# A first softmax in two pieces with a share on GpSimd, a first y copied by PSUM banks, and one softmax piece moved forward

## The chip, the cores and the metric

The kernel runs on one core of one Trainium2 chip. The metric is the device time in microseconds (us), the median over runs of one launch. The engines are TensorE (PE; its weight loads are PEld), VectorE (DVE), ScalarE (ACT), GpSimd (POOL) and SyncE (SP, which here only issues DMAs).

## The reference, cut to what matters

A causal dynamic convolution with softmax weights over 7 taps, 8 heads of 24 columns, then two dense layers with a squared ReLU between them.

```python
w = softmax(weight_gen, axis=-1)              # (8, 4096, 8 heads, 7 taps)
out[b, s, h, :] = sum_k w[b, s, h, k] * x_pad[b, s + k, h, :]
h = np.maximum(out.reshape(32768, 192) @ w_in, 0.0)       # 192 x 2048
result = h * h @ w_out                                    # 2048 x 192
```

## The kernel before

The sequence is cut into blocks of 512 or 1024 positions. For each block, DVE multiplies rows of softmax weights (`wr`) by a mask into band matrices (`bd`). PE multiplies bands by x into PSUM (`yp`), and a copy to `y` follows. PE then multiplies y by `w_in` into `h`, ACT takes ReLU to `t`, DVE squares to `g`, and PE multiplies by `w_out` into `o`. ACT copies and DVE adds `o` into `o_sb`. The first softmax part covers the first 1024 positions.

```python
        def exp(self, lo, hi):            # ACT
            ...
            nc.scalar.activation(out=self.ex[:, lo:hi]..., in_=self.wg[:, lo:hi]..., func=ActF.Exp)

        def total(self, lo, hi):          # DVE: sums over the taps
            nc.vector.tensor_reduce(out=self.ssum[:, lo:hi]..., in_=self.ex[:, lo:hi]..., ...)

        def scale(self, lo, hi, eng):
            while lo < hi:
                n = min(SL - lo % SL, hi - lo)
                for g in range(HP):       # 4 pairs of heads
                    eng.tensor_tensor(out=..., in0=self.ex[:, lo : lo + n, g],
                                      in1=self.rcp[:, lo : lo + n, g]..., op=AluOp.mult)
                lo += n
...
        # st_conv(j): the first y is copied in three pieces, two of them of one bank
            copies = ((k0, k1, nc.scalar.copy),)
            if j == 0:
                copies = ((0, 1, nc.scalar.copy),) + tuple(
                    (k, k + 1, nc.vector.tensor_copy) for k in range(1, NK)
                )
...
        s0.load(nc.sync)                                  # weights of the first softmax
        load_w_in(w_st[0], 0, nc.sync)
        x_load_f32(0)
        load_w_in(w_st[1], 1, nc.sync)
        s0.exp(0, s0.rh)
        s0.total(0, s0.rh)
        s0.recip(0, s0.rh)
        s0.scale(0, s0.rh, nc.vector)
        nc.scalar.copy(out=w_i[:, 0, 0], in_=w_st[0])
        wr_load_sbuf(0, [s0], (0, 2, 1, 4, 3), (nc.sync, nc.gpsimd))   # moves of softmax rows
        wr_load_sbuf(1, [s0], range(NT), (nc.gpsimd,))
        x_cast(0, nc.scalar.copy)
        cross_w_in_by_pe(0)
        spin(14)                                          # matmuls that keep the clock up
        x_load_f32(1)
        nc.scalar.copy(out=w_i[:, 1, 0], in_=w_st[1])
        cross_w_in(1)
        s1.load(nc.sync)
        for i in (0, 2, 1, 3, 4):
            st_band(0, (i,))
        st_conv(0)
...
        # later: plans say after which unit ("u") an exp (E), a softmax piece (S),
        # bands (B), a half of the second layer (M) or the next convolution (C) comes
            3: "L5 L6 M S3 u u u M u u u u M u M B6 E4 u u u M M B7 u u u M u M C S4 u",
...
        TIMES = {
            (1, 0): ((3, 15), (4, 1)),    # part 4: second piece after unit 1 of block 4
```

The softmax here doesn't subtract the row's maximum and nothing guards it: scores larger than these inputs give would overflow.

## Time and profile before

| | |
|---|---|
| time, median of 4 runs | 748.41 us (747.88 to 750.02) |
| span of the profiled run | 746.1 us |
| PE busy | 738.3 us, 99% |
| chain that ended last | 94% PE, 3% DVE, 1% each DMA and ACT |
| DVE, ACT, POOL busy | 621.9, 624.1, 88.9 us |
| first matmul of the second layer | 25.82 us |
| PE's one shown wait for an engine after that | 0.48 us at 89.29 us |

A busy PE is not a PE at its peak, but what an edit can win without touching matmuls lies where PE waits. The prediction shows those places. Two of them count here: the start, where a chain of single steps leads to the first convolution, and one wait near 89 us. In a line of the timeline the two first numbers are start and length, and the bracket at the end is the engine's idle time ahead of it and what ended that time.

### The profile page before, as it was taken

What the parts mean: (1) busy time and instruction counts of PE and PEld (TensorE: products, weight loads), DVE (VectorE), ACT (ScalarE), POOL (GpSimd) and SP (SyncE); (2) the same over time, 40 slices, a digit from 0 to 9 for tenths busy, and PEclk for the clock granted to TensorE, in tenths of its full rate; (3) what the DMA queues carried; (4) which work ended last, traced back from release to release, by engine and by line L of the source; (5) the groups of instructions that cost most, each with busy time, mean ns of one, the idle gap of its engine ahead of it and who ended that gap; (6) DMA issues with size and microseconds to landing.
All of it is one profiled execution on the core that took longest, in us unless ns stands there. A gap on an engine that the chain in (4) does not pass through costs nothing.

```text
span 746.1 us, 33290 instructions
## 1 busy us (share of the span) xinstructions
PE 738.3 (99%) x15106; PEld 558.0 (75%) x15106; DVE 621.9 (83%) x1003; ACT 624.1 (84%) x755; POOL 88.9 (12%) x130
## 2 busy tenths in 40 slices
PE   8999999999999999999999999999999999999998
PEld 4767777777777797777877777787777777777787
DVE  5999898998889888887889888898888987677853
ACT  5998888898888888888888888888888888888884
POOL 7322220101101100011000110001100011000000
PEclk9999999999999999999999999999999999999999
DMA  8755444435554244643146442265341354442312
GB/s 218 118 100 115 80 93 93 99 71 139 94 118 80 72 59 80 140 83 71 39 78 139 98 69 61 43 139 108 59 80 47 58 108 80 60 73 51 51 45 66
DMA packets 122170, 64.81 MB, mean 87 GB/s; under 512 B 83850, under 2 KB 118637, under 8 KB 121517
## 3 DMA queue, kind: packets, MB, share of 16 engines
q1 hardware_dynamic: 77708, 45.66, 22.3%
q0 software_dynamic: 44176, 16.93, 20.1%
q8 instruction: 118, 1.93, 1.0%
q14 instruction: 24, 0.19, 0.1%
q10 hardware_dynamic: 144, 0.10, 0.0%
HBM read 48.61 MB, written 28.70 MB: 104 GB/s over the span
## 4 chain that ended last, share of the span: by engine, by line
PE 94%; DVE 3%; DMA 1%; ACT 1%; issue 1%; DVEq 0%; ACTq 0%
PE o L482 45%; PE h L448 43%; PE yp L416 6%; DVE bd L348 1%; DVE g L460 1%; DMA wr<-v_first 0%; DMA wg<-in_weight_gen_dram 0%; ACT t L457 0%; DVE v_first L239 0%; DVE ssum L224 0%; DVE rcp L231 0%; ACT ex L217 0%; DVE o_sb L498 0%; ACT y L434 0%; ACT o_sb L496 0%
## 5 line engine op out<-in xcount | busy, mean ns | idle before, releaser
L457 ACT ACTIVATE t<-h 128x1024 f16<-128x1024 f32 x512 | 496.7, 1026 | 64.8 <-PE h L448 64.4
L460 DVE TENSOR_TENSOR g<-t 128x1024 f16<-128x1024 f16 x512 | 333.9, 686 | 99.6 <-ACT t L457 97.0
L482 PEld LDWEIGHTS <-g 64*128 64x128 f16 (+1 forms) x8032 | 351.5, 94 | 55.0 <-issue 4.1
L482 PE MATMUL o<-w_o,g 64*128 64x192 f16 (+1 forms) x8032 | 383.9, 243 | 0.5 <-DVE o_sb L498 0.5
L448 PE MATMUL h<-y,w_i 64*128 64x512 f16 (+1 forms) x3168 | 378.7, 370 | 1.7 <-ACT t L457 0.8
L448 PEld LDWEIGHTS <-w_i 64*128 64x128 f16 x3168 | 163.5, 94 | 114.8 <-issue 5.0
L348 DVE TENSOR_TENSOR bd<-wr,mask 128x4160 f16<-128x4160 f16 (+3 forms) x89 | 149.3, 1701 | 3.7 <-DMA wr<-v_first 3.7
L300 POOL DMA_DIRECT2D xt<-in_x_dram x62 | 51.6, 836 | 443.0 <-PE yp L416 420.1
L496 ACT COPY o_sb<-o 128x384 f32<-128x384 f32 x129 | 62.3, 483 | 33.9 <-PE o L482 33.9
L498 DVE TENSOR_TENSOR o_sb<-o,o_sb 128x384 f32<-128x384 f32 x123 | 68.2, 554 | 8.4 <-ACT o_sb L496 5.6
L434 ACT CAST y<-yp 128x1024 f16<-128x1024 f32 (+1 forms) x64 | 47.7, 796 | 15.0 <-PE yp L416 15.0
L416 PE MATMUL yp<-bd,xt 128*32 128x104 f16 (+8 forms) x3864 | 51.8, 208 | 0.6 <-DVE bd L348 0.3
L416 PEld LDWEIGHTS <-xt 128*32 128x32 f16 (+3 forms) x3864 | 46.1, 91 | 7.0 <-issue 6.4
L217 ACT ACTIVATE ex<-wg 128x448 f32<-128x448 f32 (+2 forms) x44 | 27.2, 618 | 1.9 <-DMA wg<-in_weight_gen_dram 1.9
L239 DVE TENSOR_TENSOR v_big<-ex,rcp 128x112 f16<-128x112 f32 (+1 forms) x136 | 27.3, 263 | 1.6 <-DMA vd<-v_big 0.4
L224 DVE TENSOR_REDUCE ssum<-ex 128x64 f32<-128x448 f32 (+2 forms) x44 | 26.1, 593 | 2.4 <-ACT ex L217 2.4
L231 DVE RECIPROCAL rcp<-ssum 128x64 f32<-128x64 f32 (+2 forms) x44 | 23.7, 539 | 1.5
L290 POOL DMA_DIRECT2D xt<-in_x_dram x7 | 3.8, 548 | 137.2 <-PE yp L416 137.2
L330 POOL DMA_DIRECT2D wr<-v_first x31 | 16.8, 559 | 18.3 <-DVE v_first L239 18.1
L546 PE MATMUL wp<-warm 128*128 128x512 f16 x39 | 10.5, 434 | 1.3 <-DVE warm L538 1.3
L546 PEld LDWEIGHTS <-warm 128*128 128x128 f16 x39 | 4.2, 110 | 6.9 <-issue 2.4
L239 DVE TENSOR_TENSOR v_first<-ex,rcp 128x112 f16<-128x112 f32 (+1 forms) x48 | 9.1, 255 | 0.3
(25 smaller groups left out, 28.6 us busy)
## 6 DMA issues: line engine op xcount, KB each, us to landing
out_dram<-o_sb SPq DMA_DIRECT2D x63, 384.0 KB, 2.9
xt<-in_x_dram POOLq DMA_DIRECT2D x42, 240.0 KB, 5.7
wg<-in_weight_gen_dram SPq DMA_DIRECT2D x4, 1064.0 KB, 8.2
xt<-in_x_dram POOLq DMA_DIRECT2D x20, 192.0 KB, 5.4
wr<-vd SPq DMA_DIRECT2D x38, 80.0 KB, 3.7
vd<-v_big SPq DMA_DIRECT2D x5, 512.0 KB, 5.5
wg<-in_weight_gen_dram SPq DMA_DIRECT2D x5, 392.0 KB
wg<-in_weight_gen_dram SPq DMA_DIRECT2D x3, 616.0 KB, 4.5
```

The lines of the kernel that those rows point to most:

```text
L217: nc.scalar.activation(out=self.ex[:, lo:hi].rearrange("p r g k e -> p (r g) k e"), in_=self.wg[:, lo:hi].rearrange("p r (g e) k -> p (r g ...
L239: eng.tensor_tensor(out=bass.AP(tensor=v.tensor, offset=v.offset + lo * H * SL + lo % SL * 2 + g * SL * 2, ap=[list(v.ap[0]), [H * SL + 2, ...
L300: eng.dma_start(out=dst[:, first:last], in_=ap)
L348: nc.vector.tensor_tensor(out=bd_t[j][:, H * lo : H * (lo + len(tiles) * n)].rearrange("p (g m c) -> p g m c", g=shape[1], c=2 * SL), in0= ...
L416: nc.tensor.matmul(out=yps[k // per][p0 : p0 + m, col + a : col + b], lhsT=x_t[s][:, i, 32 * q : 32 * q + m], rhs=bd[:, h // 2, h % 2, a - ...
L434: copy(out=y[:, a:b, 0:th], in_=yp[:, (a - k0) * th : (b - k0) * th].rearrange("p (k c) -> p k c", c=th),)
L448: nc.tensor.matmul(out=h[:, half, jj * th : (jj + 1) * th], lhsT=w_in_chunk(u * per + jj, slot, half), rhs=y_t[j][r0 : r0 + RT, k, 0:th], ...
L457: nc.scalar.activation(out=t1, in_=h, func=ActF.Relu)
L460: nc.vector.tensor_tensor(out=g, in0=t1, in1=t1, op=AluOp.mult)
L482: nc.tensor.matmul(out=oo[:, cc * Dm : (cc + 1) * Dm], lhsT=g[r0 : r0 + n, cc * P : (cc + 1) * P], rhs=w_o[r0 : r0 + n, fc, :], start=(fc ...
L496: nc.scalar.copy(out=o_sb, in_=o[0][:, c])
L498: nc.vector.tensor_tensor(out=o_sb, in0=o[1][:, c], in1=o_sb, op=AluOp.add)
```

## The change

It means to shorten the start and take away that wait. The sums begin after the first part of exp (8 of the 14 rows that a partition holds) instead of after all of it, GpSimd does a quarter of the scaling, ACT and DVE each copy one PSUM bank of the first y, and the second piece of part 4's softmax comes one unit sooner.

```diff
-        def scale(self, lo, hi, eng):
+        def scale(self, lo, hi, eng, pairs=range(HP)):
...
-                for g in range(HP):
+                for g in pairs:
...
-                copies = ((0, 1, nc.scalar.copy),) + tuple(
-                    (k, k + 1, nc.vector.tensor_copy) for k in range(1, NK)
-                )
+                copies = ((0, 2, nc.scalar.copy), (2, NK, nc.vector.tensor_copy))
...
-        s0.exp(0, s0.rh)
-        s0.total(0, s0.rh)
+        for lo, hi in ((0, FIRST), (FIRST, s0.rh)):
+            s0.exp(lo, hi)
+            s0.total(lo, hi)
         s0.recip(0, s0.rh)
-        s0.scale(0, s0.rh, nc.vector)
+        s0.scale(0, s0.rh, nc.vector, range(HP - 1))
+        s0.scale(0, s0.rh, nc.gpsimd, (HP - 1,))
...
-            3: "... M M B7 u u u M u M C S4 u",
+            3: "... M M B7 u u u E4 M u M C S4 u",
...
-            (1, 0): ((3, 15), (4, 1)),
+            (1, 0): ((3, 15), (4, 0)),
```

## The prediction

> **What bounds the kernel now.** I read the page first, its busy shares and the chain of work that ended last.
>
> ```profile
> PE 738.3 (99%) x15106; PEld 558.0 (75%) x15106; DVE 621.9 (83%) x1003; ACT 624.1 (84%) x755; POOL 88.9 (12%) x130
> PE 94%; DVE 3%; DMA 1%; ACT 1%; issue 1%; DVEq 0%; ACTq 0%
> ```
>
> The span is 746.1 us, and 94% of the chain is TensorE (PE): two dense layers, back to back. The edit leaves every matmul as it is. It can only win where PE waits, so I looked for PE's holes with the table of busy time by stretch: PE is busy 8.10 of the 10 us from 15 to 25, 9.52 of 10 us from 80 to 90, and 579.96 of 580 us from 140 to 720. The first 25 us, which include the fill, and one hole near 89 us are all that is on offer. The end, 23.18 of 26 us, isn't touched.
>
> Next, the chain of waits in order of time through the start; columns are start, length, what.
>
> ```profile
> 0.82 3.13 DMA wg<-in_weight_gen_dram
> 3.98 0.94 ACT ex L217
> 4.94 0.98 DVE ssum L224
> 5.95 0.86 DVE rcp L231
> 6.83 1.47 DVE v_first L239 x8
> 8.31 3.57 DMA wr<-v_first
> 11.98 2.61 DVE bd L348 x5
> ```
>
> Every step is serial: the load, exp, sums, reciprocal, scaling, the move of rows, then the bands that the first convolution multiplies by. Lastly the timeline of the first y copy and what follows, by engine.
>
> ```profile
> 15.11 0.37 ACT L434 CAST y<-yp 128x256 f16<-128x256 f32 x1 [1.94 <-PE yp L416]
> 15.51 0.75 DVE L434 CAST y<-yp 128x256 f16<-128x256 f32 x2 [0.93 <-ACT y L434]
> 15.99 2.91 PE L448 MATMUL h<-y,w_i 64*128 64x256 f16 x47 [0.19 <-DVE y L434]
> 16.97 2.85 ACT L457 ACTIVATE t<-h 128x1024 f16<-128x1024 f32 x3 [1.49 <-PE h L448]
> ```
>
> VectorE (DVE) starts its copies when ScalarE (ACT) has ended its own: they share a bank for the second third of y. PE gets its y piecewise and stalls between. From 16.97 ACT runs without a hole until 27.8 us; PE waits for it at 21.61 and then takes over as the bound at 25.06, where the chain turns into PE alone. So the start saves what the first ACT pass on h, now at 16.97, moves forward.
>
> The hole near 89 us, again in the timeline:
>
> ```profile
> 79.57 0.69 DVE L460 TENSOR_TENSOR g<-t 128x1024 f16<-128x1024 f16 x1 [0.49 <-ACT t L457]
> 81.34 0.69 DVE L460 TENSOR_TENSOR g<-t 128x1024 f16<-128x1024 f16 x1 [1.08 <-ACT t L457]
> ...
> 88.69 0.55 DVE L498 TENSOR_TENSOR o_sb<-o,o_sb 128x384 f32<-128x384 f32 x1
> 89.29 1.48 PE L482 MATMUL o<-w_o,g 64*128 64x192 f16 x31 [0.48 <-DVE o_sb L498]
> ```
>
> DVE idles 1.08 us before 81.34, then runs two softmax pieces (82.58 to 84.3 and 84.83 to 87.0) that delay its o_sum at 88.69. PE waits 0.48 us for it. ACT's half of that o_sum ended by 87.31 (86.83 + 0.48), so DVE is at fault.
>
> **What the Trainium skill says.** "SBUF — State Buffer", section "Who interferes with whom": a DVE instruction with two SBUF inputs contends with a GpSimd instruction that reads SBUF, and the loser blocks. The split scaling is exactly this pair. No GpSimd instruction with two inputs is in this trace, so it neither agrees nor disagrees. "GPSIMD Engine Reference", section "3.1 Elementwise — side-by-side cycle accounting", gives 4497 ns for a tensor_tensor add of 2048 fp32 elements; again there is none here. "PSUM — Partial Sum Buffer", section "PSUM bank collisions raise a hardware error", has it that two engines may not be in the same bank and quadrant at once. The trace agrees as far as it can: DVE sat idle 0.93 us until ACT's y copy had ended. "DMA: Bandwidth & Descriptors", section "Queues, rings and completion order", says that a DMA engine consumes one ring's descriptors in order. The trace fits: the first row move landed after 3.57 us, behind the large weight loads of the same queue, where moves from the softmax buffer take 1.7 us at least and 2.2 in the median over the first 30 us.
>
> **The change, part by part.**
>
> Exp and sums in two pieces. By the rows with shapes kept apart, 448 elements of exp take 633 ns and 336 take 525; the sums take 608 and 494. ACT's instructions overlap by some 0.11 us (three of 1.026 in 2.85) and DVE's scaling ones by some 0.08. Exp ends at 3.98 + 0.63 = 4.61 and at 4.61 - 0.11 + 0.53 = 5.03. The first sums run from 4.63 to 5.24, the second from 5.16 to 5.65. The reciprocal starts at about 5.68 for 5.95 and the scaling at 6.58 for 6.83: 0.25 us won.
>
> Scaling shared with GpSimd. DVE keeps 6 of 8 instructions: 1.47 x 6/8 = 1.10 us, so it ends at 7.68 for 8.30. GpSimd gets one of 112 and one of 84 elements. My estimate from the GPSIMD page: 4497/2048 = 2.2 ns an element, plus 0.1 us each for starting (its 1-element memsets take 0.10 in the trace), gives 0.35 + 0.28 = 0.63 us. It clears v_big until 6.99 (4.55 + 2.44), so alone it would end at 7.62. If each blocks the other fully, both end at 6.58 + 1.10 + 0.63 = 8.31, and the saving of the first part is lost. I take the middle, 8.0: the row moves are issued 0.3 us earlier.
>
> Does the landing follow? The large piece of the second weight half is issued at 4.07 and lands 6.9 us later, at 10.97; the first rows land at 11.88. The DMA engines are at 90% or more from 5.5 to 9.6 us. I let half through: bands start 0.15 us earlier. The warming matmuls ahead of the convolution don't eat this: the last of 14 starts at 12.79, and PE then waits for bands (0.28 us at 14.13).
>
> The y copy by banks. ACT copies 512 columns, 592 ns by its row of that shape, from 15.11 to 15.70, and DVE the other bank from 15.11 to 15.53. The first h then starts at 15.73 with all of y. Before, its first matmul stood at 15.53, the next at 15.99, and the third pair of operands was only there at 16.27 (15.51 + 0.75 and some). A pass of 12 such matmuls takes 0.76 in the chain; 15.73 + 0.76 = 16.49, with 0.15 us to reach ACT 16.64 for 16.97: 0.33 us won. DVE comes free 0.7 us earlier too, but the second convolution's y copy isn't waiting for it, because ACT is busy.
>
> The softmax piece of part 4. Its exp (525 ns) moves into the block before, where ACT has a hole of 0.84 us, and its sums, reciprocal and scaling one unit forward. They take 1.72 us (82.58 to 84.3) and now fall into DVE's idle 1.08 us. DVE's o_sum at 88.69 comes about 1.1 us earlier, 87.6, and is gated then by ACT at 87.31. PE wanted it at 88.81 (88.57 + 0.24), so the whole 0.48 us goes; I count 0.45.
>
> Sum: 0.15 + 0.33 + 0.45 = 0.93 us of 748.18, or 747.2.
>
> **The rivals.** First, the port pair: GpSimd and DVE block each other, the scaling ends at 8.3 or later, and part one is worth nothing. For it speaks the skill; against it, GpSimd starts late, with part of DVE's work done. It leaves 747.4. Second, the row moves are hidden behind the weight loads whatever the softmax does; the 10.97 landing speaks for it, that moves are short and the loads nearly drained by 9.6 against it. This too gives 747.4. Third, ACT meets the next softmax load: the part-1 weights are requested at 14.40 as before and exp starts at 19.70 without a shown wait. If they land only shortly before, the y copy's 0.33 us turns into a wait there, giving 747.6 or so. Fourth, the softmax shift: if the earlier exp or the later g (0.7 us at 81.34) makes PE wait elsewhere, some 0.3 us returns. If all that is good goes right (rows follow fully, GpSimd is unhindered: 0.6 for 0.15), 746.7.
>
> **Range and chances.** Mechanisms span about 746.7 to 748.2. The three runs of before lie from 747.88 to 750.02, so a median can be off by some tenths. I predict 747.2 us, with 746.1 to 748.4 holding it 8 times in 10. Two per cent would be 15 us; PE's idle time in the whole span is 746.1 - 738.3 = 7.8 us, so faster by over 2% is out of reach (0.005), and nothing in the edit can add 15 us (0.005): within 2%, 0.99.
>
> **What would show it.** Of the changed kernel: scaling ends between 7.7 and 8.3, with GpSimd's two instructions from about 7.0; the first row move still lands near 11.7; DVE's single y copy starts with ACT's at about 15.0; the first ACT pass on h starts near 16.5 and PE's unbroken stretch 0.5 us earlier than 25.06; PE no longer waits for o_sum near 89 us, and DVE's idle 1.08 us is filled. The prediction is wrong if a new PE wait stands in blocks 3 to 5, if the landing moves by a whole half microsecond or goes back, or if exp of part 1 shows a DMA wait.

## The result

| | before | after |
|---|---|---|
| time, median of 4 runs | 748.41 us | 747.93 us (747.22 to 748.56) |
| ratio | | 0.9990, 95% interval 0.9972 to 1.0008 |
| span of the profiled run | 746.1 us | 746.3 us |

The ratio is the mean time of one kernel's runs over that of the other's runs of the same rounds, so it isn't quite the ratio of the medians. Its interval contains 1: the time alone doesn't show a gain. The traces have to.

The page of the changed kernel, busy shares and chain:

```profile
PE 738.4 (99%) x15106; PEld 560.4 (75%) x15106; DVE 622.1 (83%) x1001; ACT 624.4 (84%) x756; POOL 89.4 (12%) x132
PE 95%; DVE 2%; ACT 1%; DMA 1%; issue 1%; DVEq 0%; ACTq 0%; SPq 0%
```

PE is the bound as before. The chain of waits through the start of the changed kernel (start, length, what):

```profile
4.14 0.63 ACT ex L217
...
4.79 1.04 DVE ssum L224 x2
...
5.86 0.86 DVE rcp L231
...
6.74 1.46 DVE v_first L239 x6
...
8.28 3.24 DMA wr<-v_first
...
11.62 2.61 DVE bd L348 x5
```

The reader should compare lengths. Six scaling instructions on DVE take 1.46 us, as eight did before (1.47), and the row move is issued at 8.28 for 8.31: exp took less, but it began 0.16 us later in this run, behind its load. Yet the bands start at 11.62 for 11.98, because the move took 3.24 us for 3.57. That difference isn't the softmax's doing, as the experiments show. The timeline of the first y copy in the changed kernel, ACT, DVE and PE:

```profile
14.74 0.58 ACT L432 CAST y<-yp 128x512 f16<-128x512 f32 x1 [1.92 <-PE yp L416]
...
15.36 0.42 DVE L432 CAST y<-yp 128x256 f16<-128x256 f32 x1 [1.15 <-ACT y L432]
...
16.49 2.85 ACT L455 ACTIVATE t<-h 128x1024 f16<-128x1024 f32 x3 [1.16 <-PE h L446]
```

DVE's copy of the second bank still begins when ACT's has ended. From the start of the y copy to the first ACT pass on h it is 16.49 - 14.74 = 1.75 us for 1.86 (16.97 - 15.11): 0.11 us won, not 0.33. Last, the place of the old wait, DVE and PE of the changed kernel:

```profile
79.40 0.69 DVE L458 TENSOR_TENSOR g<-t 128x1024 f16<-128x1024 f16 x1 [0.51 <-ACT t L455]
80.01 0.50 DVE L224 TENSOR_REDUCE ssum<-ex 128x48 f32<-128x336 f32 x1
...
93.40 0.55 DVE L496 TENSOR_TENSOR o_sb<-o,o_sb 128x384 f32<-128x384 f32 x1
...
93.63 1.85 PE L480 MATMUL o<-w_o,g 64*128 64x192 f16 x32
```

The softmax piece now runs at 80.01 in what was an idle stretch, and PE's wait at 89 is gone. But a group of 32 matmuls that takes 1.48 us elsewhere takes 1.85 at 93.63: PE waits there for DVE's o_sum at 93.40, behind two bands. In the terms of the 0.48 us of before this is 0.13 us of idle time: the group's first matmul ends at 93.87 and the next starts at 94.00.

Both kernels keep the same instructions from the sixth block on. From its convolution (the *arrival*, 99.19 us before and 98.67 after) to the last block's, the trace has 609.81 us before and 610.66 after. So the changed kernel came 0.52 us sooner to the steady stretch and lost 0.85 us in it, which is why its span is no shorter. The 0.52 us add up, to 0.01: the first matmul of the second layer came 0.46 us sooner (25.36 for 25.82), the fifth block took 0.32 us less, and the fourth, from its convolution to the fifth's, took 0.25 more (22.85 for 22.60). That loss in the fourth block doesn't belong to the change: the second trace of the changed kernel has 22.60 there (e10).

### The profile page after: what moved, and what is told of

The parts are those of the page before. It is cut to its first block, busy times and chain, and to the rows that moved or that the text cites. A ratio compares the mean times of both kernels' runs of the same rounds, so it can differ in the third digit from the quotient of the medians.

```text
span 746.3 us, 33293 instructions
## 1 busy us (share of the span) xinstructions
PE 738.4 (99%) x15106; PEld 560.4 (75%) x15106; DVE 622.1 (83%) x1001; ACT 624.4 (84%) x756; POOL 89.4 (12%) x132
## 4 chain that ended last, share of the span: by engine, by line
PE 95%; DVE 2%; ACT 1%; DMA 1%; issue 1%; DVEq 0%; ACTq 0%; SPq 0%
PE o L480 45%; PE h L446 43%; PE yp L416 6%; ACT t L455 1%; DVE bd L348 1%; DMA wg<-in_weight_gen_dram 0%; DMA wr<-v_first 0%; DVE g L458 0%; ACT ex L217 0%; DVE v_first L239 0%; DVE ssum L224 0%; DVE o_sb L496 0%; DVE rcp L231 0%; ACT y L432 0%; DVE y L432 0%
## 5 line engine op out<-in xcount | busy, mean ns | idle before, releaser
L446 PEld LDWEIGHTS <-w_i 64*128 64x128 f16 x3168 | 166.2, 94 | 112.8 <-issue 4.1
```

Source lines behind the costliest of these rows:

```text
L446: nc.tensor.matmul(out=h[:, half, jj * th : (jj + 1) * th], lhsT=w_in_chunk(u * per + jj, slot, half), rhs=y_t[j][r0 : r0 + RT, k, 0:th], ...
```

## The experiments

Twelve experiments ran, on two chips. Each is given by its difference from the changed kernel unless said otherwise. A table of what the traces show comes first; all times are us from the start of the span. "Weights" is the landing of the large piece of the second weight half, "rows" the issue of the first row move on SP, "bands" the start of the first band. "y to h" runs from the start of the y copy to ACT's first pass on h, "fifth" from the fifth block's convolution to the sixth's, "steady" from the arrival to the last convolution.

| kernel | weights | rows | bands | y to h | fifth | arrival | steady |
|---|---|---|---|---|---|---|---|
| before | 11.02 | 8.31 | 11.98 | 1.86 | 23.24 | 99.19 | 609.81 |
| before again (e8) | 11.95 | 8.33 | 12.85 | 1.86 | 23.26 | 100.02 | 610.86 |
| after | 10.36 | 8.28 | 11.62 | 1.75 | 22.92 | 98.67 | 610.66 |
| after again (e10) | 10.89 | 8.20 | 12.14 | 2.17 | 22.90 | 99.90 | 610.99 |
| e1, scaling on DVE | 10.51 | 8.09 | 11.80 | 1.74 | 22.90 | 98.51 | 611.91 |
| e2, two y tiles | 10.76 | 8.08 | 11.66 | 1.50 | 22.92 | 98.62 | 611.92 |
| e3, no shift | 11.05 | 8.11 | 11.97 | 1.74 | 23.18 | 99.14 | 611.33 |
| e6, e1 and e2 together | 10.65 | 8.30 | 11.83 | 1.50 | 22.92 | 98.33 | 610.33 |
| e12, e6 again | 10.94 | 8.10 | 11.89 | 1.51 | 22.91 | 98.31 | 610.35 |
| e7, scaling on GpSimd | 11.11 | 9.63 | 11.82 | 1.74 | 22.91 | 99.32 | 610.09 |

### e1 and e7: who does the scaling

Theory: the two engines block each other, so GpSimd's quarter buys nothing. Rival: it helps, and something else hid it.

```diff
-        s0.scale(0, s0.rh, nc.vector, range(HP - 1))
-        s0.scale(0, s0.rh, nc.gpsimd, (HP - 1,))
+        s0.scale(0, s0.rh, nc.vector)        # e1
+        s0.scale(0, s0.rh, nc.gpsimd)        # e7
```

> The changed kernel with the whole first scaling back on VectorE (8 instructions), all else kept. Theory (the two engines block each other, GpSimd's share is bought back in full): from the start of the first exp to the end of the scaling 4.05 us as with the split, +-0.05, because 8 unhindered VectorE instructions take 1.45 us and 6 hindered ones took 1.45 too; GpSimd issues its first row move about 0.3 us after the scaling instead of 0.67. Rival (the split does help, something else in that run hid it): the scaling takes 0.2 to 0.4 us longer than with the split. Time within 0.5 us of the changed kernel either way.

> The changed kernel with the whole first scaling on GpSimd, VectorE idle: it measures GpSimd's instruction by itself. Theory (with the split, each engine was blocked while the other read): GpSimd's instruction of 112 elements takes 0.33 to 0.40 us from start to start, that of 84 0.26 to 0.32, for 0.45 with the split; the whole scaling about 2.7 us. Rival (GpSimd isn't blocked, it is simply this slow, and only VectorE was blocked): 0.45 us from start to start. Time not asked.

The groups of instructions around the scaling, shapes kept apart (busy us, mean ns of one). First the changed kernel, GpSimd and DVE:

```profile
L239 POOL TENSOR_TENSOR v_first<-ex,rcp 128x112 f16<-128x112 f32 x1 | 0.5, 478 | 0.0
L239 POOL TENSOR_TENSOR v_first<-ex,rcp 128x84 f16<-128x84 f32 x1 | 0.4, 360 | 0.0
...
L239 DVE TENSOR_TENSOR v_first<-ex,rcp 128x112 f16<-128x112 f32 x3 | 0.8, 336 | 0.0
L239 DVE TENSOR_TENSOR v_first<-ex,rcp 128x84 f16<-128x84 f32 x3 | 0.7, 280 | 0.0
```

e1, DVE alone:

```profile
L239 DVE TENSOR_TENSOR v_first<-ex,rcp 128x112 f16<-128x112 f32 x4 | 0.8, 270 | 0.0
L239 DVE TENSOR_TENSOR v_first<-ex,rcp 128x84 f16<-128x84 f32 x4 | 0.7, 240 | 0.0
```

e7, GpSimd alone:

```profile
L239 POOL TENSOR_TENSOR v_first<-ex,rcp 128x112 f16<-128x112 f32 x4 | 1.4, 387 | 0.0
L239 POOL TENSOR_TENSOR v_first<-ex,rcp 128x84 f16<-128x84 f32 x4 | 1.2, 342 | 0.0
```

DVE's instruction is longer when GpSimd works: 336 ns for 270 on average. In the changed kernel the stretching stands instruction by instruction: DVE's third takes 464 ns while GpSimd's first runs, and its fourth 377 for 240 while GpSimd's second runs. GpSimd's first is longer too in this trace, 478 ns for 387. But in the second trace of the changed kernel (e10), where DVE's third and fourth took 464 and 379 ns again, it is not:

```profile
L239 POOL TENSOR_TENSOR v_first<-ex,rcp 128x112 f16<-128x112 f32 x1 | 0.4, 392 | 0.0
L239 POOL TENSOR_TENSOR v_first<-ex,rcp 128x84 f16<-128x84 f32 x1 | 0.4, 360 | 0.0
```

So DVE is held up in both traces, and GpSimd not in each: that the two block each other is shown for one side only. From the start of exp to the end of the scaling it is 4.05 us with the split, 4.06 on DVE alone (e1) and 4.31 before. So two pieces of exp gave 0.25 us, and GpSimd gave nothing. In e7 GpSimd's instructions start 0.35 and 0.29 us apart and the whole scaling takes 2.62 us, near the 2.7 that the theory had.

The split has a small cost too: GpSimd's first row move follows the scaling by 0.67 us with it, by 0.31 before and by 0.31 in e1. In the first trace of the changed kernel DVE waited 0.57 us for the second block's rows, which are all moved by GpSimd. The other traces of this order with the split (e2, e3 and e10) have no such wait, so it isn't a steady cost.

The time of e1 was 748.03 us for 748.93 before, ratio 0.9992 (0.9977 to 1.0007), unclear as was expected.

### Does the landing follow? e4, e7 and e8

Theory: the first rows queue behind the weights on the DMA engines, so a softmax that ends sooner gains nothing. Rival: the landing follows the issue, wholly or by half as the prediction had it. e4 issues the second weight half behind the first three row moves.

```diff
         x_load_f32(0)
-        load_w_in(w_st[1], 1, nc.sync)
...
         wr_load_sbuf(0, [s0], (0, 2, 1, 4, 3), (nc.sync, nc.gpsimd))
+        load_w_in(w_st[1], 1, nc.sync)
```

> The changed kernel with the load of the second weight half issued behind the three first row moves of the same queue. It is a test of what sets the landing of the rows; it should cost time, as the weights then come late (0.5 to 2 us). Theory (the rows queue behind the weight loads): first row move lands 2.0 to 2.6 us after its issue for 3.24 and 3.57. Rival (a move of 128-byte rows takes 3.2 us by itself): 3.0 us or more.

The timeline of DVE, the line of the first bands, in e4:

```profile
10.27 2.60 DVE L348 TENSOR_TENSOR bd<-wr,mask 128x832 f16<-128x832 f16 x5 [2.17 <-DMA wr<-v_first]
```

In e7, where the rows are issued 1.5 us later than in e1:

```profile
11.82 2.60 DVE L348 TENSOR_TENSOR bd<-wr,mask 128x832 f16<-128x832 f16 x5 [5.19 <-DMA wr<-v_first]
```

In e8, the kernel before run again:

```profile
12.85 2.60 DVE L348 TENSOR_TENSOR bd<-wr,mask 128x832 f16<-128x832 f16 x5 [4.54 <-DMA wr<-v_first]
```

With the weights out of the way the first move lands 2.0 us after its issue and bands start at 10.27. With the weights ahead, bands start at 11.82 whether the rows are issued at 9.63 (e7) or near 8.1 (11.80 in e1). In e8 the same program as before, its rows issued at 8.33, has its weights 0.93 us later and its bands 0.87 us later. The weights of e7 landed even later than those of e1 (11.11 for 10.51), so they can't have made up for the late issue. So the end of the softmax has about 1.5 us of slack in this pair, and the 0.36 us by which the changed kernel's bands came sooner go with weights that landed 0.66 us sooner in that one run. They don't go with the issue: among the nine traces of the table that issue the rows from 8.08 to 8.33, an issue at 8.28 has the soonest bands (11.62) and one at 8.10 has 11.89. Nor do they follow the weights to the tenth: from landing to bands it is 0.71 to 1.29 us. The prediction's second rival is shown.

e4 cost 6 us (754.94, ratio 1.0083, 1.0069 to 1.0096), more than the 0.5 to 2 expected: ACT converts the late weights ahead of the y copy, which then began at 17.98 us, and PE, idle meanwhile, had a granted clock of 0.50 from 18 to 21 us.

> The kernel before, unchanged, as if it were a change: it shows what two sets of runs of one program differ by, and a second trace of it. Expected: ratio 1.000 with an interval of some +-0.15%, so that a gain of 0.4 us (0.05%) can't be seen in the time; landing of the weights' large piece and of the first rows moved together by up to 0.4 us against the first trace; 1.86 us from the y copy's start to the first pass on h and PE's wait near 89 us as before; PE's losses after 100 us different from the first trace by up to 1 us.

e8 gave 749.39 us against 749.16 of the same program in the same rounds, ratio 1.0009 (0.9995 to 1.0022): two sets of one program can differ by 0.09%, or 0.7 us. In its trace the start moved by 0.9 us where 0.4 was expected.

### e2: why DVE waits with its y copy

The program as built has DVE's copy wait on an ACT semaphore, although the two copies read different banks. Both read one PSUM tile. e2 gives each bank a tile.

```diff
+        if j == 0:
+            per = 2                     # one PSUM tile for each bank
         yps = [
             ps_h.tile([P, 2 * TB], f32, name="yp", tag="h") for _ in range(-(-NK // per))
         ]
...
-                copies = ((0, 2, nc.scalar.copy), (2, NK, nc.vector.tensor_copy))
+                copies = ((k0, k1, (nc.scalar.copy, nc.vector.tensor_copy)[n]),)
```

> The changed kernel with the first y's two banks as two PSUM tiles instead of one, copies as before. Theory (VectorE waits for ScalarE because both copies read one tile, not because of a bank): VectorE's copy now starts with ScalarE's (within 0.1 us), PE's first dense matmuls run without the wait for the third part of y, and the first ScalarE pass on h starts 0.25 to 0.3 us sooner after the end of the convolution: about 1.5 us after it for 1.77. Rival (the two engines' reads are kept apart for the y tile they write, or the pass waits for something else): no change, 1.77 us. Whole time 0.3 us less at most, which the timing hardly shows.

The program as built now has that copy wait on PE. The timeline of ACT and DVE in e2:

```profile
14.75 0.58 ACT L434 CAST y<-yp 128x512 f16<-128x512 f32 x1 [1.92 <-PE yp L418]
16.25 1.94 ACT L457 ACTIVATE t<-h 128x1024 f16<-128x1024 f32 x2 [0.92 <-PE h L448]
...
14.81 0.42 DVE L434 CAST y<-yp 128x256 f16<-128x256 f32 x1 [0.55 <-PE yp L418]
```

DVE now starts 0.06 us after ACT, and it is 1.50 us to the first pass on h: 0.25 less than with one tile and 0.36 less than before. The rival falls: it was neither a bank nor the y tile. The time was 749.02 us, ratio 1.0000 (0.9987 to 1.0013). The trace shows part of why: PE later waited for bands near 33 us, whose rows landed until 29.6 us in this run. What held them was not tested.

### e3: the softmax shift

```diff
-            3: "... M M B7 u u u E4 M u M C S4 u",
+            3: "... M M B7 u u u M u M C S4 u",
-            (1, 0): ((3, 15), (4, 0)),
+            (1, 0): ((3, 15), (4, 1)),
```

> The changed kernel with the second exp and softmax piece of part 4 back where they were. Theory: PE's wait of 0.48 us for o_sum near 88 us returns, VectorE's idle 1.08 us returns before it, and the stretch from one convolution to the next there takes 23.2 us for 22.9. Rival (that wait was gone for the earlier start of everything, or chance): no PE wait there. Time up by 0.3 to 0.5 us, near what the timing resolves.

The timeline of PE in e3:

```profile
89.24 1.48 PE L480 MATMUL o<-w_o,g 64*128 64x192 f16 x31 [0.41 <-DVE o_sb L496]
```

The wait returns, and with it 23.18 us for the fifth block. Three traces without the shift have 23.18 to 23.26 there, all eleven with it 22.90 to 22.94: 0.32 us between the two means. The wait that vanished was 0.41 to 0.48 us; 0.13 us of it came back as the idle time near 94 us, in all eleven traces. The time, 749.81 us and ratio 1.0016 (1.0002 to 1.0030), is worse than this accounts for: 1.2 us by the ratio, where the trace explains 0.3. Its steady stretch was 1.5 us longer than that of the first trace of before, with the same instructions.

### e6 and e12: scaling on DVE with two y tiles

> As the last, without moving the weight pieces: scaling on VectorE, the first y in two PSUM tiles. It asks whether the 0.5 us that the two-tile run lost after its better start (bands of the third block waited for rows until 29.6 us) is its own or chance. Theory (chance, the loads of that stretch were late in that one run): first pass on h 1.5 us after the y copy's start again, and no wait of PE for bands near 33 us; arrival at the sixth block's convolution 98.2 to 98.4. Rival (the earlier VectorE work makes GpSimd's loads late): the loss of about 0.5 us near 33 us is back, arrival 98.6 or later.

> The version with the scaling on VectorE and the first y in two PSUM tiles again, to see whether its gain over the kernel before repeats: ratio 0.998 to 1.000, 1.5 us from the y copy's start to the first pass on h, arrival at the sixth block's convolution 98.2 to 98.7. If it is 1.000 or more the first ratio of 0.9986 was chance.

Both traces reach the sixth block at 98.33 and 98.31, sooner than any trace of the two kernels, with 1.50 us from the y copy to h. PE had no wait near 33 us, so e2's loss there was chance, or at least isn't bound to two tiles. The times: 747.60 us with ratio 0.9986 (0.9972 to 0.9999), then 748.22 with 0.9997 (0.9982 to 1.0013). The gain over the kernel before is seen in both traces, and in the times in one set of two.

### e5, e9 and e11: rows ahead of a part of the weights

These start from e6 and try to collect the 1.5 us that the rows wait. e5 issues only the two small pieces (256 KB) of the second weight half behind the row moves. e9 also issues the next exp load sooner and converts the small part after the y copy. e11 also loads the third block's x later.

```diff
-        load_w_in(w_st[1], 1, nc.sync)
+        load_w_in(w_st[1], 1, nc.sync, 0)          # e5: large piece
...
         wr_load_sbuf(0, [s0], (0, 2, 1, 4, 3), (nc.sync, nc.gpsimd))
+        load_w_in(w_st[1], 1, nc.sync, 1)          # e5: small pieces
...
+        s1.load(nc.sync)                           # e9: here, not after the next two
-        nc.scalar.copy(out=w_i[:, 1, 0], in_=w_st[1])
-        cross_w_in(1)
-        s1.load(nc.sync)
+        nc.scalar.copy(out=w_i[:, 1, 0, 0:NQ], in_=w_st[1][:, 0:NQ])
...
         st_conv(0)
+        nc.scalar.copy(out=w_i[:, 1, 0, NQ:], in_=w_st[1][:, NQ:])
+        cross_w_in(1)
...
-        x_load(2)                                  # e11: moved behind S1's row moves
```

> All of the scaling on VectorE, the first y in two PSUM tiles, the softmax shift kept, and the two small pieces (256 KB) of the second weight half issued behind the three first row moves of the queue instead of ahead of them; ScalarE converts the large and the small part of that half one after the other. Theory (rows queue behind weight bytes, some 0.7 us for 256 KB at 370 GB/s): first bands start 0.5 to 0.9 us sooner than the 11.6 to 12.0 of the runs so far, that is 10.9 to 11.3; the first ScalarE pass on h near 15.7; arrival at the convolution of the sixth block (98.5 to 99.2 so far) near 98.0. Rival (only the large piece matters, or the warming matmuls and the copies hold the convolution back): bands or y copy where they were. Whole time 0.5 to 1.3 us under the kernel before, at the edge of what the timing resolves.

> As the run with the two small weight pieces behind the row moves, mended: the exp load of the next softmax part is issued before the copies between halves of the weights, and ScalarE converts the small weight part after the first y copy, not before it. Theory (that run lost 4 us because ScalarE waited for that load until 21.4 us and PE, idle for 3.9 us, then got half its clock): first bands near 10.3 again, first pass on h near 15.4, no wait of ScalarE for the exp load over 0.5 us, granted clock 1.0 throughout, arrival at the sixth block's convolution 97.3 to 98.0. Rival (the weights' halves come too late whatever the order): PE waits for the second weight half or ScalarE for the load by over 1 us, arrival 99 or later.

> As the run with the mended order, with the input of the third block (432 KB) loaded behind GpSimd's second set of row moves instead of ahead of it. That run reached its first second-layer matmul at 24.68 us, 0.7 us sooner than any other, and then lost about 1 us near 33 us to rows landing at 28.3 to 30.4. Theory (those rows queue behind loads too): rows of part 1 all landed by 28.8 us, no wait of PE over 0.2 us near 33, arrival at the sixth block's convolution 97.6 to 98.2. Rival (other traffic holds them, or the later input makes the third convolution wait instead): arrival 98.8 or later.

In all three the bands start at 10.20 to 10.37 us, more than the theory's 0.7 us sooner. In e5, busy time by stretch (PE, PEld, DVE, ACT and POOL busy, then PE's granted clock, DMA share, GB/s) shows what that turned into:

```profile
20.00:22.00 2.00, 0.00 (x0) 0.00 (x0) 0.00 (x0) 0.52 (x1) 0.61 (x1) 1.00 1.38 237
...
24.00:26.00 2.00, 2.00 (x22) 1.67 (x20) 1.97 (x10) 1.90 (x3) 0.00 (x0) 0.50 1.36 295
```

ACT waited 2.85 us for the next softmax's load, which SP had issued behind the late weights. PE idled 3.86 us, from 19.52, and its clock was 0.50 from 22.4 to 29.2 us; the first second-layer matmul came at 29.58 us. e5 took 749.94 us, ratio 1.0022 (0.9999 to 1.0045). e9 mended that and had this matmul at 24.68, the soonest of all, then lost the gain again (timeline of PE):

```profile
33.76 1.86 PE L419 MATMUL yp<-bd,xt 128*32 128x104 f16 x118 [0.99 <-DVE bd L349]
```

The third block's bands waited for rows that landed from 28.3 to 30.4 us. Arrival was 99.18, where the rival of that run had it, but the cause was the rows and not the weights or the exp load (ACT waited 0.78 us for that): 748.69 us, ratio 1.0000 (0.9985 to 1.0015). In e11 those rows had landed by 28.5, but PE now waited 0.93 and 0.22 us for the copies between the weight halves, and its clock fell to 0.50 again: 748.32 us, ratio 0.9993 (0.9978 to 1.0008), arrival 99.66. In all three the wait only moved from one transfer to another. None of them reached the sixth block as soon as e6 and e12, and by the times e9 and e11 can't be told from these.

### e10: the changed kernel again

> The changed kernel again, for a second trace and more times. Expected: scaling 1.45 us with GpSimd's two instructions inside it, the y copy of VectorE behind ScalarE's, 1.75 us from the y copy's start to the first pass on h, PE waits 0.1 to 0.2 us near 94 us and not near 89, first bands 0.8 to 1.3 us after the large weight piece lands, as in the other runs; ratio to the kernel before 0.9985 to 1.0005.

Ratio 0.9991 (0.9977 to 1.0006), 748.41 us for 748.33: again no gain clear of the noise. The waits stood where they were expected except one: 2.17 us from the y copy to h for 1.75. In this trace the granted clock was 0.54 from 16 to 18 us, which no other trace of a kernel with this order shows. The bands were also 0.52 us later than in the first trace. The arrival, 99.90, was 1.23 us later; how much of that each made is not shown.

## Why the prediction was right, and where its steps were not

The time, 747.93 us, fell within the range, and the class was right. Part of this is luck. The range also held 748.18, the time of no gain at all, and the second set of runs of the same kernel (e10) had a median of 748.41. The predicted 0.93 us came from three terms, 0.15, 0.33 and 0.45, all of them oversized. ACT's first pass on h stood at 16.49, exactly where the first two terms put it (16.97 - 0.15 - 0.33), but for other reasons: the y copy began 0.37 us sooner, with the weights of that one trace, and 0.11 came from the copy itself.

- **Exp and sums in two pieces, 0.25 us.** Right in itself: 4.06 us for 4.31 from exp to the end of the scaling, with the scaling on DVE. By the third point it reached nothing.
- **Scaling shared with GpSimd, the middle of two extremes.** The number was near: counted from the exp of before, the scaling ends at 3.98 + 4.05 = 8.03 us for the predicted 8.0. DVE's six instructions took 1.46 us for 1.10, so GpSimd's 0.63 us cost DVE 0.36 and not all. The first rival, by which exp's 0.25 us would be lost too, doesn't hold. But the step wasn't compared with eight instructions on DVE alone, which end as soon (4.06 us in e1): GpSimd's share bought nothing. The estimate of GpSimd's own cost was near: 0.35 and 0.28 us, measured 0.35 and 0.29 from start to start.
- **"I let half through".** This step failed. Nothing gets through: rows issued 1.5 us later gave the same bands. The second rival holds, and the term of 0.15 us is 0; the 0.36 us of the first trace go with the weights, whose landing scatters from run to run.
- **The y copy by banks, 0.33 us.** The mechanism was taken for a matter of banks, so the step "DVE the other bank from 15.11" failed: the copies of one tile are ordered by a semaphore of the program. It gave 0.11 us. With a tile for each bank the same reckoning gives 0.36, which shows the cause.
- **The softmax piece of part 4, 0.45 us.** The mechanism is right and the size was off: 0.32 us. The fourth rival took 0.13 us, as a wait for o_sum near 94 us. A new PE wait in blocks 3 to 5 was one of the prediction's own signs of being wrong.

One sum of the prediction is off: its best case is 748.18 - 0.60 - 0.33 - 0.45 = 746.8, not 746.7. The sum of what the runs show is 0 + 0.11 + 0.32 = 0.43 us. The medians differ by 0.48, and the two ratios mean 0.7; all agree, but neither interval excludes zero. The main reason is the steady stretch: the same instructions took 609.81 to 611.92 us in the ten traces of the table. Some of its slow blocks hold PE gaps of 0.1 to 0.4 us for which the profile shows no waiting instruction; they make up only a part of the difference. What causes these is open, and no run tested it. Open too is what delays GpSimd's first row move after a split scaling.

## What to carry to other kernels

A step on the chain of waits is worth shortening only if the next step waits for it: ask what a transfer queues behind, and delay its issue once on purpose to see. Two engines read one accumulator side by side only if the program's dependencies let them, so look at what the second one waits on, not only at the banks. When an edit is worth less than the scatter of the time, count it where it acts, stretch by stretch over several traces, and repeat the unchanged kernel to know the scatter.

## What the Trainium skill lacked or had wrong

- "SBUF — State Buffer", section "Who interferes with whom": agrees that the two contend. DVE's instruction of 112 elements took 336 ns on average for 270 with GpSimd beside it; GpSimd's took 478 for 387 in one trace of the changed kernel and 392 in the other. The page has no numbers for instructions this short.
- "GPSIMD Engine Reference", section "3.1 Elementwise — side-by-side cycle accounting": its figure of 4497 ns for 2048 elements scaled well. Measured start to start: 0.35 us for 112 elements and 0.29 for 84. No page has the 0.67 us between a split scaling and GpSimd's next DMA issue, for 0.31 otherwise.
- "DMA: Bandwidth & Descriptors", section "Queues, rings and completion order": agrees. A move of 16 KB took 2.0 us with nothing large ahead and 3.2 to 4.4 when it was issued near 8.2 us behind 768 KB of weights. It lacks a warning that loads in flight set the floor for small moves issued later.
- "PSUM — Partial Sum Buffer", section "PSUM bank collisions raise a hardware error": nothing here contradicts it, but it leads one to think by banks, while the built program orders two engines' copies of one tile: 1.75 us for 1.50 with two tiles.
- "TensorE: Matmul & The Clock Gate", section "Part 1: The HAM clock gate (the "warmup" mystery)", gives half clock after an idle window of some 3.4 us. In e4 and e5 the clock fell in waits of 4.61 and 3.86 us, but already some 2.0 and 2.8 us after the last matmul. In e10 it fell after shown waits of 0.28, 0.28 and 0.67 us and in e11 after 0.15, 0.93 and 0.22, while in e7 it stayed at 1.00 through a wait of 1.77. No run tells why.
